# Transformer block on one core: the order of POOL and ScalarE work in the up phase of token block 1

## The chip, the core and the metric

The kernel runs on one core of a Trainium2 chip. The core has five engines with instruction queues of their own, which run in order and wait for one another by semaphores: TensorE (PE in the profile; its weight loads are PEld), VectorE (DVE), ScalarE (ACT), GpSimd (POOL) and SyncE (SP), which here issues transfers. The metric is the device time of one launch in microseconds; the kernel before takes 1042.02 us, the median of three runs (1041.74 to 1042.28).

## What is computed

An attention without softmax, a normalisation per head, and a gated feed-forward block, all in fp32:

```
kv  = einsum('bhsd,bhse->bhde', k, v)          # 8 batches, 8 heads, 576 tokens, 64 columns
o   = einsum('bhsd,bhde->bhse', q, kv)
x   = o / sqrt(mean(o*o) + 1e-6) * g_norm      # per head; then 4608 tokens x 512
g   = x @ w_gate;  val = x @ w_val             # 512 -> 1536
out = (silu(g) * val) @ w_out                  # 1536 -> 512
```

## The kernel before, in words

The 4608 tokens are nine blocks of 512. A block has an up phase (`Ffn.up`: x times w_gate and w_val, and h = silu(g) * val) and a down phase (`Ffn.down`: h times w_out), between and inside which the attention of the next block is woven. Products are done by Strassen's scheme in Winograd's form: seven products instead of eight, at the price of sums of operands and results. Block 0's up phase is plain. Block 1 (the only one with `0 < n < DEEP`, DEEP being 2) uses one level, in six units of class `Up`, called pairs here, 0 to 5: each makes 256 of the 1536 columns of h. Blocks 2 to 8 use two levels (`Inner`), with weight sums that block 1 prepares and writes to DRAM ("leaf steps").

A pair has products P1, P5, P4, P3, P6, P2, P7; each is eight records of 128x256 on PE. `sequence` puts a pair's P4 and P3 behind the P1 and P5 of the next pair. So on PE the order is P1(j+1), P5(j+1), P4(j), P3(j), P6(j+1), P2(j+1), P7(j+1), and what lies from one P1 to the next is called a slot here; slot j is the one in which h of pair j is made. After pairs 1 and 3 there is also a product of k and v, and after pair 5 there are transposes of q for block 2, since there is no next pair.

P1, P6, P7 and P4 add up in one PSUM bank (`b`), which is read out between them: by ACT copies after P1 (L526), P6 (L530) and P7 (L560), and by ACT's silu after P4 (L566). P5 and P3 do so in bank `c`, which VectorE reads (L111) after P7 and after P3. P2 is in bank `a`; VectorE adds it to the copy of P1 (`after2`), and ACT's silu of that sum is L561. Then h is two products on POOL (L113): the first from P4's silu, "h a" below, the second from the sum after P3, "h b". VectorE's `h_sums` makes two further sums of them for the down phase, the second of which needs h b; they are `s<-h` and `h<-s,h` in the profile.

Three of the seven weight operands of a pair are differences T, made on POOL by `Up.prepare` (L112, `t<-wv`, `t<-wg,wv`), for P5, P7 and P4. Their tiles come from a pool of nine. VectorE's leaf steps then work on the same tiles in place and their results go to DRAM; only then may a tile be used again, three pairs later. The down phase has three such differences of w_out for each of P5, P7 and P4 (`turn_t`, `t<-wo`).

The program's text doesn't fix the order on an engine: a scheduler does, by when it takes operands to be ready. `tc.issue_after(ins)` puts what is traced inside it behind `ins` in the queue of the engine of `ins`, and changes nothing on other engines.

In the order before, ACT has in each pair the silu of L561 ahead of the copy of L560. POOL has T of pair 3 before and between the two h products of pair 0, T of pair 4 about those of pair 1, T of pair 5 about those of pair 2, and the T of the down phase's P5 about those of pair 3.

Of the kernel before, what the change touches and what calls it, by code (L numbers as in the profile page):

```python
# [12 lines left out]
ACT = mybir.ActivationFunctionType  # L13
# [5 lines left out]
def kernel(  # L19
# [41 lines left out]
    nc = tc.nc  # L61
# [5 lines left out]
    BLK = P * T  # L67
    HB = BLK // 2
# [4 lines left out]
    NP = NF // 2  # L73
# [39 lines left out]
    mul = lambda e, o, a, b: e.tensor_tensor(out=o, in0=a, in1=b, op=OP.mult)  # L113
# [371 lines left out]
    DEEP = 2  # L485
# [3 lines left out]
    class Quad:  # L489
# [8 lines left out]
        def prepare(self):  # L498
            pass
# [32 lines left out]
    class Up(Quad):  # L532


        def __init__(self, ffn, j):
            super().__init__(2)
            self.ffn, self.j = ffn, j
            self.h = ffn.h[:, 2 * j : 2 * j + 2]

        def prepare(self):  # L540
            j = self.j
            b11, b21, t2, b22 = wg[j][:, 0:2], wg[j][:, 2:4], wv[j][:, 0:2], wv[j][:, 2:4]
            t = []
            for b in (b22, b11, b21):
                t.append(t_tile())
                sub(nc.gpsimd, t[-1], b, t2)
            self.w = {1: b11, 2: b21, 3: b22, 6: t2, 5: t[0], 7: t[1], 4: t[2]}
# [9 lines left out]

        def after7(self):
            self.u3 = self.piece(2)
            nc.scalar.copy(out=self.u3, in_=self.ps["b"])  # L560
            nc.scalar.activation(out=self.s, in_=self.s, func=ACT.Silu)  # L561
            add(nc.vector, self.u3, self.ps["c"], self.u3)

        def after4(self):
            g = self.piece(3)
            nc.scalar.activation(out=g, in_=self.ps["b"], func=ACT.Silu)  # L566
            mul(nc.gpsimd, self.h[:, :, HB:BLK], g, self.u3)

        def after3(self):
            add(nc.vector, self.u2, self.ps["c"], self.u2)  # L570
            mul(nc.gpsimd, self.h[:, :, 0:HB], self.s, self.u2)
            self.ffn.ended = self.ffn.h_sums(self.j, 1, nc.vector)

        def multiply(self, p):
# [180 lines left out]
    def t_tile(key=None):  # L755

        stream.held.append(key)
        return t_pool.tile([P, 2, 2 * P], F32, name="t")
# [114 lines left out]
    class Ffn:  # L873
# [22 lines left out]
        def up(self, fill):  # L896

            self.s1 = s_pool.tile([P, NP, HB], F32, name="s1")
            units = []
            for d in range(NP // 2):  # L900
                if self.n < DEEP:
                    units += [Up(self, 2 * d), Up(self, 2 * d + 1)]
                else:
                    shared = {}
                    units += [Inner(self, d, g, shared) for g in range(4)]
            units[0].prepare()
            last = None
            for i, this in enumerate(units):
                if i + 1 < len(units):
                    units[i + 1].prepare()  # L910
                for unit, p in this.sequence(last):
                    if unit:
                        unit.multiply(p)
                        self.make(4)
                last = this
                fill.get(12 * (i + 1) // len(units), lambda: None)()
            self.down_ = Down(self)
            self.down_.turn_t(5)
            for unit, p in last.sequence(None):
                if unit is None:  # L920
                    last.multiply(p)
# [159 lines left out]
```

## Time and profile before

| | before |
|---|---|
| time, median of three | 1042.02 us |
| span of the profiled run | 1040.8 us |
| VectorE busy | 702.9 us, 68% |
| ScalarE busy | 230.9 us, 22% |
| POOL busy | 369.3 us, 35% |
| granted TensorE clock, mean of the run | 0.994 |

The profile has a page for the whole run, and views that can be asked of a stretch of it: the timeline of an engine, a table of who waited for whom, and a table of busy times by stretch. In a timeline the columns are the start in us, the length in us (including a wait for a resource in the engine itself), engine, line, operation, output and input, and a number of merged instructions; a bracket gives idle time ahead of it and what ended it. Lines L111, L112 and L113 are one-line helpers for add, subtract and multiply, so tile names and not lines tell such instructions apart: `r` is working room, `t` the tiles of T, `wv`, `wg`, `wo` the weights, `s` and `h` the sums and h. Block 1's up phase, the stage concerned, is from 162.5 to 247.8 us.

### The profile page before, as it was taken

What the parts mean: (1) busy time and instruction counts of PE and PEld (TensorE: products, weight loads), DVE (VectorE), ACT (ScalarE), POOL (GpSimd) and SP (SyncE); (2) the same over time, 40 slices, a digit from 0 to 9 for tenths busy, and PEclk for the clock granted to TensorE, in tenths of its full rate; (3) what the DMA queues carried; (4) which work ended last, traced back from release to release, by engine and by line L of the source; (5) the groups of instructions that cost most, each with busy time, mean ns of one, the idle gap of its engine ahead of it and who ended that gap; (6) DMA issues with size and microseconds to landing.
All of it is one profiled execution on the core that took longest, in us unless ns stands there. A gap on an engine that the chain in (4) does not pass through costs nothing.

```text
span 1040.8 us, 21533 instructions
## 1 busy us (share of the span) xinstructions
PE 1015.1 (98%) x8588; PEld 911.7 (88%) x8588; DVE 702.9 (68%) x1203; ACT 230.9 (22%) x356; POOL 369.3 (35%) x280
## 2 busy tenths in 40 slices
PE   5899999999999999999999999999999999999998
PEld 4644688788899989998999899988999899989997
DVE  2999596888655866665766656683668566856661
ACT  2666211122212121111111121211222121212110
POOL 0000443435024631563046305540355126512670
PEclk9899999999999999999999999999999999999999
DMA  9787303765467556764677377726862666066611
GB/s 244 216 268 248 107 1 115 189 187 154 120 184 239 141 102 196 245 164 77 197 238 196 58 205 226 221 47 169 247 194 56 157 207 190 30 152 209 192 31 41
DMA packets 255043, 168.15 MB, mean 162 GB/s; under 512 B 124640, under 2 KB 230240, under 8 KB 254944
## 3 DMA queue, kind: packets, MB, share of 16 engines
q1 hardware_dynamic: 229536, 163.63, 55.6%
q10 hardware_dynamic: 25344, 3.15, 1.9%
q8 instruction: 68, 1.11, 0.4%
q14 instruction: 31, 0.25, 0.1%
q0 software_dynamic: 64, 0.00, 0.0%
HBM read 138.02 MB, written 22.41 MB: 154 GB/s over the span
## 4 chain that ended last, share of the span: by engine, by line
PE 91%; DVE 4%; DMA 2%; SPq 1%; issue 1%; POOL 0%; ACT 0%; DVEq 0%; POOLq 0%; ACTq 0%
PE b L659 25%; PE b L510 20%; PE c L659 12%; PE c L510 9%; PE a L659 6%; PE a L510 5%; PE b L953 4%; PE c L953 4%; PE m L285 2%; PE m L326 1%; SPq L228 1%; DVE xi L112 1%; DMA w<-t 1%; PE m L373 1%; DMA ld<-in_moe_w_gate_dram 1%
## 5 line engine op out<-in xcount | busy, mean ns | idle before, releaser
L111 POOL TENSOR_TENSOR r<-r 128x256 f32<-128x256 f32 (+1 forms) x105 | 110.8, 1061 | 309.3 <-DVE r L111 263.0
L111 DVE TENSOR_TENSOR r<-b,r 128x512 f32<-128x512 f32 (+1 forms) x273 | 162.0, 606 | 63.6 <-PE b L659 59.1
L112 POOL TENSOR_TENSOR t<-wo 128x512 f32<-128x512 f32 x81 | 115.6, 1451 | 196.7 <-DVE wo L111 108.1
L111 DVE TENSOR_TENSOR r<-c,r 128x512 f32<-128x512 f32 (+1 forms) x179 | 108.5, 617 | 89.1 <-PE c L659 49.3
L659 PE MATMUL b<-x,t 128*128 128x128 f32 x1092 | 151.0, 276 | 0.0
L111 DVE TENSOR_TENSOR r<-a,r 128x512 f32<-128x512 f32 (+1 forms) x99 | 62.5, 631 | 110.7 <-PE a L510 65.8
L659 PEld LDWEIGHTS b<-x,t 128*128 128x128 f32 x1092 | 136.5, 192 | 0.6 <-DVE r L111 0.2
L113 POOL TENSOR_TENSOR h<-r 128x1024 f32<-128x1024 f32 (+1 forms) x40 | 81.5, 2052 | 87.4 <-DVE r L111 74.1
L659 PE MATMUL c<-xi,t 128*128 128x128 f32 x840 | 112.2, 275 | 0.3 <-DVE xi L111 0.3
L659 PEld LDWEIGHTS c<-xi,t 128*128 128x128 f32 x840 | 102.8, 192 | 0.4 <-DVE xi L111 0.4
L510 PE MATMUL b<-wo,h 128*128 128x256 f32 x432 | 99.4, 382 | 0.1
L510 PE MATMUL b<-t,h 128*128 128x256 f32 x432 | 96.9, 381 | 0.0
L510 PEld LDWEIGHTS b<-t,h 128*128 128x128 f32 x432 | 81.4, 190 | 11.2 <-issue 0.2
L510 PEld LDWEIGHTS b<-wo,h 128*128 128x128 f32 x432 | 80.0, 190 | 12.6 <-DVE h L113 2.5
L673 ACT COPY r<-b 128x512 f32<-128x512 f32 x63 | 36.9, 585 | 212.7 <-PE b L659 205.9
L659 PE MATMUL b<-xi,t 128*128 128x128 f32 x588 | 79.7, 276 | 0.0
L659 PEld LDWEIGHTS b<-xi,t 128*128 128x128 f32 x588 | 72.4, 192 | 0.0
L659 PE MATMUL b<-x,wg 128*128 128x128 f32 x336 | 52.7, 279 | 0.2 <-DVE x L112 0.2
L659 PE MATMUL b<-x,wv 128*128 128x128 f32 x336 | 51.4, 276 | 0.0
L510 PE MATMUL c<-t,s 128*128 128x256 f32 x216 | 48.3, 380 | 0.0
L510 PE MATMUL a<-wo,h 128*128 128x256 f32 x216 | 48.3, 379 | 0.0
L510 PE MATMUL c<-wo,h 128*128 128x256 f32 x216 | 48.1, 379 | 0.0
(131 smaller groups left out, 1591.1 us busy)
## 6 DMA issues: line engine op xcount, KB each, us to landing
t<-w SPq DMA_DIRECT2D x336, 256.0 KB, 3.3
out_dram<-r SPq DMA_DIRECT2D x17, 512.0 KB, 3.1
ld<-in_moe_w_gate_dram SPq DMA_DIRECT2D x12, 512.0 KB, 4.9
ld<-in_moe_w_val_dram SPq DMA_DIRECT2D x12, 512.0 KB, 4.8
ld<-in_moe_w_out_dram SPq DMA_DIRECT2D x12, 512.0 KB, 4.5
w<-t SPq DMA_DIRECT2D x18, 256.0 KB, 2.4
w<-xi SPq DMA_DIRECT2D x12, 384.0 KB, 3.2
ld<-in_k_dram SPq DMA_DIRECT2D x26, 160.0 KB, 3.5
```

What stands on the lines that cost most here:

```text
L111: add = lambda e, o, a, b: e.tensor_tensor(out=o, in0=a, in1=b, op=OP.add)
L112: sub = lambda e, o, a, b: e.tensor_tensor(out=o, in0=a, in1=b, op=OP.subtract)
L113: mul = lambda e, o, a, b: e.tensor_tensor(out=o, in0=a, in1=b, op=OP.mult)
L228: nc.sync.dma_start(out=t, in_=src[self.n, 2 * j : 2 * j + 2, s0 : s0 + m * D].rearrange("h (p t) d -> p h (t d)", t=m),)
L285: nc.tensor.matmul(self.kv_ps[r][u * D : (u + 1) * D, j, :], lhsT=self.k[j, r][:, u, c, :], rhs=self.v[j, r][:, u, c, :], start=(c == 0), ...
L326: nc.tensor.matmul(self.ps[i][u][p : p + D, t, j, :], lhsT=self.qt[rows, 2 * i + t, j, p : p + D], rhs=kvs[b % 3][rows, j, :], start=True, ...
L373: nc.tensor.transpose(ps[:, e, t], xt[:, t, j + e], ident)
L510: nc.tensor.matmul(banks[e][:, e], lhsT=lhsT, rhs=rhs, start=first and i == 0 and (e == 0 or banks[0] is not banks[1]), stop=i == self.ste ...
L659: nc.tensor.matmul(ps[:, i, f], lhsT=self.weight(o, p, f), rhs=self.operand(o, p), start=first and (i, f) == (0, 0), stop=True, skip_group ...
L673: nc.scalar.copy(out=dst, in_=ps)
L953: nc.tensor.matmul(t, lhsT=w[f // 2][:, i, P * (f % 2) : P * (f % 2 + 1)], rhs=x[:, i, of], start=(i == 0), stop=(i == NS - 1),)
```

## The change

Four edits, all for block 1 alone. T of a pair is no longer prepared one unit ahead of the loop but traced after P3 of the previous pair, and queued on POOL behind that pair's second h product. The T of the down phase's P5 waits, by a semaphore, for the last h sum that was made when it is traced, which is pair 4's. The silu of L561 is queued on ACT behind the copy of L560. The h products of the last pair are on VectorE. They are meant to let h go first on POOL, and to let the copy of P7 leave bank `b` without waiting for the sum that the silu needs.

```diff
@@ class Up
             self.h = ffn.h[:, 2 * j : 2 * j + 2]
+            self.engine = nc.gpsimd if j + 1 < NP else nc.vector
...
-            nc.scalar.copy(out=self.u3, in_=self.ps["b"])
-            nc.scalar.activation(out=self.s, in_=self.s, func=ACT.Silu)
+            copied = nc.scalar.copy(out=self.u3, in_=self.ps["b"])
+            with tc.issue_after(copied.ins):
+                nc.scalar.activation(out=self.s, in_=self.s, func=ACT.Silu)
...
-            mul(nc.gpsimd, self.h[:, :, HB:BLK], g, self.u3)
+            mul(self.engine, self.h[:, :, HB:BLK], g, self.u3)
...
-            mul(nc.gpsimd, self.h[:, :, 0:HB], self.s, self.u2)
+            self.made = mul(self.engine, self.h[:, :, 0:HB], self.s, self.u2)
@@ Ffn.up
-                if i + 1 < len(units):
-                    units[i + 1].prepare()
                 for unit, p in this.sequence(last):
                     if unit:
                         unit.multiply(p)
                         self.make(4)
+                    if p == 3 and i + 1 < len(units):
+                        with tc.issue_after(last.made.ins) if last and self.n < DEEP else ExitStack():
+                            units[i + 1].prepare()
...
-            self.down_.turn_t(5)
+            self.down_.turn_t(5, self.ended if self.n < DEEP else None)
```

On the engines the scheduler makes of it: POOL has T0, T1, h of pair 0, T2, h of pair 1, T3, h of pair 2, T4, h of pair 3, T5, h of pair 4, then the three T of the down phase's P5 (T0 is pair 0's three differences, and so on). ACT has copy and silu exchanged in all six pairs. VectorE's order is the same as before up to the last pair, where the two h products come in. TensorE's order is the same.

## The prediction

> **What bounds the kernel now.** I read the page first.
>
> ```profile
> PE 1015.1 (98%) x8588; PEld 911.7 (88%) x8588; DVE 702.9 (68%) x1203; ACT 230.9 (22%) x356; POOL 369.3 (35%) x280
> PE 91%; DVE 4%; DMA 2%; SPq 1%; issue 1%; POOL 0%; ACT 0%; DVEq 0%; POOLq 0%; ACTq 0%
> ```
>
> TensorE is the bound, and only its idle time or a slower clock can change the end. Next, busy times by stretch: the middle row is block 1's up phase, its neighbours the down phases beside it.
>
> ```profile
> core 0: us, PE busy (x) PEld busy (x) DVE busy (x) ACT busy (x) POOL busy (x), PEclk, DMA share, GB/s
> 120.00:162.50 42.50, 42.50 (x328) 37.49 (x327) 33.65 (x52) 9.08 (x17) 19.53 (x13) 1.00 0.14 41
> 162.50:247.80 85.30, 79.77 (x498) 68.91 (x497) 72.11 (x148) 17.61 (x32) 30.80 (x23) 0.98 0.63 175
> 247.80:288.80 41.00, 41.00 (x314) 36.00 (x313) 28.29 (x49) 7.61 (x14) 10.80 (x7) 1.00 0.47 120
> ```
>
> Only this stage loses PE time. A product takes 1.73 us from start to start in PE's timeline; 42 of them are 72.5, two k-v products of 1.31 make 2.6, transposes 0.8 and 1.1: 77.0 us. The stage takes 85.3, so about 8 us is to be had, no more. The table of waits of the stage says where:
>
> ```profile
> PE b L510 <- ACT r L560: 5.5, 3, 2.3
> PEld b L510 <- ACT r L560: 4.5, 2, 2.7
> DVE h L112 <- POOL h L113: 5.4, 2, 2.7
> POOL t L112 <- DMA w<-t: 33.2, 6, 10.0
> ```
>
> P4 waits for the copy of P7, three times; weight loads wait with it (the same time). VectorE waits twice for h, where POOL has it behind a T that waits for a tile. PE's timeline at the longest wait:
>
> ```profile
> 198.61 1.89 PE L510 MATMUL c<-x,t 128*128 128x256 f32 x8
> 202.79 3.47 PE L510 MATMUL b<-x,t 128*128 128x256 f32 x8 [2.29 <-ACT r L560]
> 206.04 2.15 PE L510 MATMUL c<-x,wv 128*128 128x256 f32 x8
> 208.03 1.89 PE L510 MATMUL b<-x,wv 128*128 128x256 f32 x8
> ```
>
> P4 came 4.18 us after P5 instead of 1.73 (2.45 lost) and then took 3.25 instead of 1.73, P3 1.99: another 1.8 us at a low clock. The two other stops (P4 at 231.81 and 243.22) lost 1.55 and 1.85 and 0.1 each afterwards. Together 7.8 us.
>
> Why is the copy late? ACT has the silu ahead of it, and that waits for VectorE's sum after P2 ("sum 2"). Sum 2 starts 1.5, 4.3, 5.8, 4.0, 4.9 and 2.4 us after P2's last start-to-start end in pairs 0 to 5. So VectorE is late, and the last view says why; VectorE's timeline, then POOL's:
>
> ```profile
> 210.98 0.41 DVE L111 TENSOR_TENSOR wv<-wv 128x256 f32<-128x256 f32 x1
> 211.42 1.64 DVE L112 TENSOR_TENSOR xi<-wv 128x512 f32<-128x512 f32 x1
> 212.98 1.49 DVE L112 TENSOR_TENSOR h<-s,h 128x256 f32<-128x256 f32 x1
> 214.40 0.41 DVE L112 TENSOR_TENSOR xi<-wv 128x256 f32<-128x256 f32 x1
> ```
> ```profile
> 211.13 1.38 POOL L113 TENSOR_TENSOR h<-r 128x512 f32<-128x512 f32 x1 [1.50 <-DVE r L111]
> 212.48 1.71 POOL L112 TENSOR_TENSOR t<-wo 128x512 f32<-128x512 f32 x1
> ```
>
> The `xi` instruction, 0.68 elsewhere, ends when POOL's h has ended; T then waits for `xi`, and `h<-s,h`, 0.41 elsewhere, for T. They take turns.
>
> **What the Trainium skill says.** SBUF — State Buffer, "Who interferes with whom": VectorE with two SBUF inputs contends with a GpSimd instruction that reads SBUF; the pair of ports is an exclusive lock, and the loser "fully blocks". With at most one SBUF input outside a two-port mode it doesn't contend. The trace agrees: the two rows above, and a VectorE copy out of PSUM at 248.97 that takes its usual 0.68 beside POOL's h. TensorE: Matmul & The Clock Gate, "What's actually happening": an idle window of about 3.4 us halves the clock, a busy one restores it. The trace agrees in kind: P4's 3.25 is nearly twice 1.73, and the low stretch cost 1.8 us; here a gap of 2.45 was already enough, ones of 1.55 and 1.85 weren't.
>
> **The change part by part.**
>
> Silu behind the copy: the copy now needs P7 and ACT alone, and is done 0.6 us after P7, while P4 comes two products (3.46 us) later. P4's waits go, up to 7.8 us. What queues behind silu now: the copy of the next P1, which P6 waits for, four products after that P1 starts; at the lags above it is in time. But P3 accumulates in bank `c`, which VectorE's sum after P7 ("sum 7") must have read. In VectorE's order sum 7 ends 2.55 us after sum 2 starts (201.0 to 203.5), against 1.87 for the old copy, and P3 is one product after P4. So the new limit on lateness is only 1.73 - 0.68 = 1.05 us looser. **The copy's wait turns into one for sum 7, if VectorE stays as late.** In the last pair, sum 7 ended at 244.47 and P3 started at 245.02: there only 0.55 can be saved.
>
> POOL's order: what VectorE pays. Its own instructions from one sum 2 to the next: pair 5's 11.31 (229.94 to 241.25) less two blocked ones (1.41 for 0.29, 1.64 for 0.68) is 9.2; pair 4's 14.42 less 1.08, 0.95, 2.72 idle for h and 0.33 for a kv sum is 9.3. I take 9.3. Each POOL instruction costs it 0.96 to 1.08 in the rows above; bounds 0.95 and the whole 1.27 of an undisturbed one; I take 1.05. Trial on before, from sum 2 of pair 0 (170.94) to the end of sum 7 of pair 5: five times 9.3, 0.3 of kv, 21 POOL instructions (11 T, 10 h) at 1.05 and 3.2 for the last stretch are 72.1; measured 73.5. So in this stage VectorE and POOL run in turns, and their sum per pair, some 14.5 us, is more than PE's 12.1.
>
> After: T2 comes into the stage (three instructions made at 154 to 159 before), T3 to T5 stay, the down phase's three T move behind pair 4's h sum, all ahead of pair 5's sum 7; h of pairs 0 to 4 is ten. That is 15 T and 10 h, 25 instead of 21: +4.2 us. T3's first instruction at 169.01, which blocked a leaf step for 0.8, goes: sum 2 of pair 0 at 170.3. In slot 0 POOL is empty until P4's silu, so VectorE, with nothing blocked, runs ahead of P5 and P4 and idles about 2.0 us (173.4 to 174.5, 175.7 to 176.5). One T lies beside sum 2 of pair 5, which reads PSUM: -0.6. Sum: 170.3 + 2.0 + 46.8 + 25 x 1.05 + 3.2 - 0.6 = 248.0 for the end of sum 7 of pair 5, 3.5 later than before. The waits for h (5.4 us) are no gain by themselves: in them POOL did instructions that VectorE now is blocked by.
>
> PE on the way: with sum 2 at about 186.7, 201.2, 215.8 and 230.7 in pairs 1 to 4, P3 stops for 0 to 2.5 us; these are repaid, since P4(5) is done at about 243 to 244.5, and P3(5) must wait for 248.0 against 245.02 before: **+3.0 us**. That stop is 3.5 to 5 us, longer than the one that cost 1.8 us of clock: **+1.8**.
>
> T in time? T of pair j+2 has its first part 3.8 us after the sum after P3 starts (210.38 to 214.2 in before), about 197.7 for pair 3, whose P5 is at 198.6; for pair 5 a stop of 0.3 us or so, inside the same slack. h on VectorE in pair 5: two of 0.68, behind sum 7, in reach of the down phase's P1, which needs them in its last sixth, 4.4 us after its start; not on the path. The down phase's T are done by 246, its P5 begins 6 us after P1: nothing. Nothing behind it changes: the down phase starts later as a whole.
>
> Sum: 1042.0 + 3.0 + 1.8 = 1046.8.
>
> **The rivals.**
>
> *TensorE becomes the bound* (chance 0.18): POOL's T fall mostly into VectorE's idle time, sum 7 is in time, and all 7.8 us come back: 1034.2. For it: h no longer waits for a T that waits for a DMA, 33.2 us of POOL's waits; the copy's wait surely goes. Against it: the trial sum, which leaves VectorE no room. A half way, some 1038, belongs here.
>
> *An exchange* (0.14): VectorE ends about where it did, because a few of the four added POOL instructions fall beside sums from PSUM, and the clock isn't lowered: sum 7 at 244.5 to 246.5, -0.5 to +1.5, near 1042.5.
>
> *The port is dearer* (0.10): in three T in a row VectorE pays the whole 1.27: 25 x 0.22 = 5.5 more at sum 7, 1052.3; half of it 1049.5.
>
> The likeliest (0.58) is 1046.8, with 1044.8 if the clock isn't lowered.
>
> **How the numbers follow.** Faster by over 0.2% is the first rival, 0.18; same the second, 0.14; slower the rest, 0.68. The range reaches down to 1038.5, to the half way of the first rival, and up to 1050, which leaves out its full gain and the upper end of the third.
>
> **What would show it.** Right: no PE wait for L560; instead PE `c` waits for VectorE `r`, longest in pair 5, 3 us or more, with slow matmuls after it; VectorE's `xi`, `wg` and `h<-s,h` behind the sum after P3 at 1.4 us instead of 0.4, one for each T; sum 7 of pair 5 near 248. Wrong: P4 and P3 back to back in all pairs, VectorE idle in slots 1 to 4, or a stage of less than 85 us. It would be wrong above all if VectorE got several instructions in between two T.

## The result and the profile after

The changed kernel takes 1046.05 us, the median of six runs (1043.85 to 1048.34), against 1042.09 us for the kernel before (1041.74 to 1042.44). The ratio is 1.0039, with a 95% interval of 1.0026 to 1.0052: slower by 4.0 us, where 1046.8 us was forecast. The two profiled runs differ by 4.3 us in their spans (1040.8 and 1045.1).

The table of waits of the changed kernel's up phase has a single row for PE. Its columns are the same as before: us in total, times, the longest.

```profile
PE c L510 <- DVE r L111: 8.8, 4, 4.4
```

The wait for the copy of P7 is gone altogether. P3, which accumulates in bank `c`, now waits for VectorE's sum 7 instead, four times. PE's timeline at the last of these, with the products around it:

```profile
240.77 1.97 PE L510 MATMUL b<-x,t 128*128 128x256 f32 x8
247.19 3.78 PE L510 MATMUL c<-x,wv 128*128 128x256 f32 x8 [4.45 <-DVE r L111]
250.76 0.63 PE L306 MATMUL b<-ident,ld 128*128 128x128 f32 x2
251.18 1.06 PE L306 MATMUL m<-ident,ld 128*128 128x128 f32 x4
252.04 0.93 PE L306 MATMUL b<-ident,ld 128*128 128x128 f32 x4
252.81 5.34 PE L510 MATMUL b<-wo,h 128*128 128x256 f32 x24
```

The same stretch before the change had no stop at P3:

```profile
243.22 1.97 PE L510 MATMUL b<-x,t 128*128 128x256 f32 x8 [1.85 <-ACT r L560]
245.02 1.89 PE L510 MATMUL c<-x,wv 128*128 128x256 f32 x8
247.84 5.34 PE L510 MATMUL b<-wo,h 128*128 128x256 f32 x24
```

P3 of pair 5 starts at 247.19 (245.02 before). Then the clock is low: from P3 to the first product of the down phase are 5.62 us, against 2.82 before (245.02 to 247.84). The down phase starts at 252.81 instead of 247.84, and the two parts of those 5.0 us are 2.2 for the wait and 2.8 for the clock. Block 2 begins 5.0 us later too (293.85 for 288.88). The spans differ by 0.7 us less than that: later, at 723 us, PE waits 0.6 us for a DMA in the profile of before, and not in that of the changed kernel.

VectorE's timeline in front of that sum 7, and POOL's:

```profile
239.96 0.41 DVE L112 TENSOR_TENSOR h<-s,h 128x256 f32<-128x256 f32 x1
240.30 0.41 DVE L112 TENSOR_TENSOR xi<-wv 128x256 f32<-128x256 f32 x1
240.63 1.49 DVE L112 TENSOR_TENSOR wg<-wg 128x256 f32<-128x256 f32 x1
242.15 1.37 DVE L111 TENSOR_TENSOR wg<-wg 128x256 f32<-128x256 f32 x1
243.45 0.68 DVE L111 TENSOR_TENSOR r<-a,r 128x512 f32<-128x512 f32 x1
244.05 1.15 DVE L112 TENSOR_TENSOR xi<-wg 128x512 f32<-128x512 f32 x1
...
246.46 0.67 DVE L111 TENSOR_TENSOR r<-c,r 128x512 f32<-128x512 f32 x1
```
```profile
240.51 4.14 POOL L112 TENSOR_TENSOR t<-wo 128x512 f32<-128x512 f32 x3 [1.02 <-PE m L306]
```

The three T of the down phase start as soon as `h<-s,h` is done (the code makes them wait for it; the bracket names a transpose on PE that ended within 0.1 us of it), and each blocks one of VectorE's next instructions: `wg` takes 1.49 and 1.37 instead of 0.41, `xi` 1.15 instead of 0.68. Sum 2 (243.45, reading bank `a` in PSUM) runs beside a T at its usual 0.68. Sum 7, the last row, ends at 247.13.

### The profile page after: what moved, and what is told of

Read it like the earlier page. It is cut to its first block, busy times and chain, and to the rows that moved or that the text cites. A ratio compares the mean times of both kernels' runs of the same rounds, so it can differ in the third digit from the quotient of the medians.

```text
span 1045.1 us, 21527 instructions
## 1 busy us (share of the span) xinstructions
PE 1015.5 (97%) x8588; PEld 911.5 (87%) x8588; DVE 706.6 (68%) x1205; ACT 231.1 (22%) x356; POOL 369.0 (35%) x278
## 4 chain that ended last, share of the span: by engine, by line
PE 90%; DVE 5%; SPq 2%; DMA 1%; issue 1%; ACT 0%; POOL 0%; DVEq 0%
PE b L662 25%; PE b L510 20%; PE c L662 12%; PE c L510 10%; PE a L662 6%; PE a L510 5%; PE c L958 4%; PE b L958 4%; PE m L285 1%; DVE xi L112 1%; PE m L326 1%; SPq L228 1%; DVE r L111 1%; DMA ld<-in_moe_w_gate_dram 1%; DVE r L112 0%
## 5 line engine op out<-in xcount | busy, mean ns | idle before, releaser
L113 POOL TENSOR_TENSOR h<-r 128x1024 f32<-128x1024 f32 (+1 forms) x38 | 79.1, 2099 | 128.1 <-DVE r L111 86.0
```

## The experiments

Theory: VectorE's instructions with two SBUF inputs and POOL's take turns, their sum per pair is more than PE's time, and the end of the up phase is set by sum 7 of pair 5. Rivals are named in the expectations. Each ratio is to the kernel before in the same batch of runs, whose level differs a little from batch to batch. The stage starts at 161.7 to 162.9 us in the profiles, so times of two kernels compare to within about 1 us, unless the shift is allowed for.

**The held silu alone.**

```diff
-            nc.scalar.copy(out=self.u3, in_=self.ps["b"])
-            nc.scalar.activation(out=self.s, in_=self.s, func=ACT.Silu)
+            copied = nc.scalar.copy(out=self.u3, in_=self.ps["b"])
+            with tc.issue_after(copied.ins):
+                nc.scalar.activation(out=self.s, in_=self.s, func=ACT.Silu)
```

> The kernel before with one edit, the silu of L561 queued behind the copy of P7; POOL and VectorE keep their order. Port theory (VectorE and POOL take turns at SBUF, so VectorE's sums are late and only the wait changes its name): P4's three waits for the copy go, and P3 waits for sum 7 instead, about 1.3 us in pair 2, 0.5 in pair 4; sum 7 of pair 5 still ends near 244.5 us, so P3 of pair 5 starts at about 244.5 instead of 245.0. Time 1041.5; if the gap of some 2.4 us in front of that P3 lowers the clock, 1043.3. Rival (the copy was the whole wait): all of the 7.8 us come back, 1034.2.

Ratio 0.9996 (0.9988 to 1.0005). PE's timeline of this kernel has the exchange of one wait for another, and the chance of the clock:

```profile
204.12 2.00 PE L510 MATMUL c<-x,wv 128*128 128x256 f32 x8 [1.70 <-DVE r L111]
...
232.96 3.44 PE L510 MATMUL c<-x,wv 128*128 128x256 f32 x8 [2.13 <-DVE r L111]
...
244.83 2.00 PE L510 MATMUL c<-x,wv 128*128 128x256 f32 x8 [0.27 <-DVE r L111]
```

P3 waits for sum 7 four times, as in the changed kernel: the rows above, for pairs 2, 4 and 5, and 0.49 us in pair 3. The stops of pairs 2 and 4 are longer than was expected, but sum 7 of pair 5 is where it was (ends 244.78; 244.47 before). What PE gained on the way is lost in front of that last sum. The copy was not the whole wait.

**The down phase's T out of the way of sum 7.**

```diff
-            add(nc.vector, self.u3, self.ps["c"], self.u3)
+            self.seven = add(nc.vector, self.u3, self.ps["c"], self.u3)
...
-            self.down_.turn_t(5, self.ended if self.n < DEEP else None)
+            self.down_.turn_t(5, last.seven if self.n < DEEP else None)
```

> The changed kernel, but the three T of the down phase's P5 wait for sum 7 of pair 5 instead of pair 4's last h sum. Port theory: the two weight sums and the xi sum that they blocked get 2.6 us back (1.49, 1.37 and 1.15 us for 0.41, 0.41 and 0.68), so sum 7 of pair 5 ends at about 244.5 instead of 247.1 and P3 of pair 5 stops for 2 us instead of 4.5. Time 1041.5 with the clock kept, up to 1043.5 if it is lowered. Rival (the loss was made earlier, by T2 to T5 in slots 0 to 3): sum 7 less than 1 us earlier, 1045 or more.

Ratio 1.0008 (0.9999 to 1.0016), against 1.0039 for the changed kernel: 3.2 us of its 4.0 are gone. PE's row for P3 of pair 5:

```profile
245.04 3.11 PE L510 MATMUL c<-x,wv 128*128 128x256 f32 x8 [1.95 <-DVE r L111]
```

Sum 7 of pair 5 ended at 244.99, 2.1 us earlier. As the stage began 0.3 us later in this profile (162.83 for 162.49), that is 2.5 us of the stage's own time, which is what the three rows of VectorE shown above were longer by. P3 took 3.11 us, so the clock still fell somewhat. The rival falls: most of the loss came from three instructions placed just ahead of sum 7.

**T written, not computed.**

```diff
-                sub(nc.gpsimd, t[-1], b, t2)
+                nc.gpsimd.memset(t[-1], 0.01)
```

> The changed kernel, but T of the six pairs isn't computed: POOL fills those tiles with a constant at the same places of its queue, which writes SBUF and reads nothing. Port theory: VectorE is blocked by ten h products and three T of w_out only, 13 instead of 25 POOL instructions; its own 9.3 us and 2.1 for h are less than the pair's 12.1 on PE, so PE has no stop in pairs 0 to 4 and a short one in pair 5: 1034 to 1037. Rival (it is the order of POOL's queue and its waits, not what POOL reads): sum 7 and PE's stops stay as in the changed kernel, 1046.

This kernel leaves out the values of T; only its times are of use. Ratio 0.9956 (0.9942 to 0.9971), 1037.5 on the scale of before, 0.5 above the range that was expected. VectorE's timeline, then POOL's, in the stretch where T of pair 2 was computed in the changed kernel:

```profile
180.98 0.41 DVE L112 TENSOR_TENSOR h<-s,h 128x256 f32<-128x256 f32 x1
181.32 0.41 DVE L112 TENSOR_TENSOR xi<-wv 128x256 f32<-128x256 f32 x1
181.65 0.41 DVE L112 TENSOR_TENSOR wg<-wg 128x256 f32<-128x256 f32 x1
```
```profile
180.45 1.45 POOL L548 MEMSET t<- 128x512 f32 x3
```

The same in the changed kernel, beside three T:

```profile
181.80 1.48 DVE L112 TENSOR_TENSOR h<-s,h 128x256 f32<-128x256 f32 x1
183.21 1.50 DVE L112 TENSOR_TENSOR xi<-wv 128x256 f32<-128x256 f32 x1
184.63 1.49 DVE L112 TENSOR_TENSOR wg<-wg 128x256 f32<-128x256 f32 x1
```
```profile
181.29 1.71 POOL L112 TENSOR_TENSOR t<-wv 128x512 f32<-128x512 f32 x1
182.97 2.87 POOL L112 TENSOR_TENSOR t<-wg,wv 128x512 f32<-128x512 f32 x2
```

Beside three fills VectorE's rows take their undisturbed 0.41. This agrees with the Trainium skill (SBUF — State Buffer, "Who interferes with whom"): a GpSimd instruction that only writes doesn't contend with VectorE's two-input ones. A fill is also shorter, 0.48 us for 1.27, but the rows show no blocking at all. P3 had no stop in pairs 0 to 4, and one of 2.9 us in pair 5, where the three T of w_out were left in.

**Unused products in the gap.**

```diff
                     last.multiply(p)
+                    if p == 4 and self.n < DEEP:
+                        spare = c_psum.tile([P, 2, HB], F32, name="c")
+                        with tc.issue_after(last.mm.ins):      # the last product of P4
+                            for i in range(8):
+                                nc.tensor.matmul(
+                                    spare[:, i % 2], lhsT=wg[0][:, i % 4, 0:P], rhs=self.att.x[:, i % 4, i // 4],
+                                    start=True, stop=True, skip_group_check=True,
+                                )
```

> The changed kernel, with eight unused products (3.5 us) on PE between P4 and P3 of pair 5, where PE stops for 4.5 us. Clock theory: P3 of pair 5 starts at 247.2 as in the changed kernel, but takes 1.9 us instead of 3.8, and the transposes and the next product run at full speed: 2 to 3 us less, 1043.2 to 1044. Rival (the stop alone costs; the slow matmuls are made up for later): 1046.

Ratio 1.0021 (1.0013 to 1.0028), 1.9 us less than the changed kernel, though PE does 3.5 us of useless work. PE's timeline:

```profile
243.44 3.62 PE L931 MATMUL c<-x,wg 128*128 128x256 f32 x16
246.89 1.89 PE L510 MATMUL c<-x,wv 128*128 128x256 f32 x8
```

P3 comes as late as in the changed kernel, but takes 1.89 instead of 3.78, and the down phase starts 2.8 us after it, at 249.71. The clock's share is thereby measured apart from the wait's, though loosely: the two ratios' intervals leave 0.3 to 3.5 us for it, an estimate from their widths.

**Single parts of the change undone.** The silu ahead of the copy again, and in another kernel the last pair's h on POOL:

```diff
-            copied = nc.scalar.copy(out=self.u3, in_=self.ps["b"])
-            with tc.issue_after(copied.ins):
-                nc.scalar.activation(out=self.s, in_=self.s, func=ACT.Silu)
+            nc.scalar.copy(out=self.u3, in_=self.ps["b"])
+            nc.scalar.activation(out=self.s, in_=self.s, func=ACT.Silu)
```
```diff
-            self.engine = nc.gpsimd if j + 1 < NP else nc.vector
+            self.engine = nc.gpsimd
```

> The changed kernel with the silu back ahead of the copy of P7; POOL's order as changed. Port theory: P4 waits for sum 2, the silu and the copy again, 1.05 us longer than P3 waits for sum 7: stops of about 2.5 us in pair 2, 1.7 in pair 3, 3.4 in pair 4 (with a lower clock after the longer ones), but in pair 5 the stop ends at the same sum: copy at 245.2, P4 then, P3 at 247.0. The end is set by VectorE's sum 7 of pair 5 and hardly moves: 1045.5 to 1047. Rival (the held silu is what made the changed kernel slow): 1042.

> The changed kernel with the last pair's h back on POOL. Port theory: these come after sum 7 of pair 5 and are in time for the last sixth of the down phase's first product either way: the same as the changed kernel, 1046 (within 0.5). Rival (two products of 0.68 us on VectorE, the short engine, cost the end 1.4 us): 1044.6.

Ratios 1.0042 (1.0027 to 1.0057) and 1.0036 (1.0023 to 1.0049): neither differs from the changed kernel's by more than the intervals. With the silu first, P4 of pair 5 waits for the copy, and so for the silu and for sum 2, until 245.38. It takes 3.75 us at a low clock, and P3 follows at 248.93, after sum 7 had ended at 247.12. So here it is sum 2 of VectorE, and not sum 7, that sets the end, at nearly the same time. The silu's place, and which engine makes the last h, are worth nothing that can be seen while VectorE is that late.

**Towards a faster version.** First, from the kernel before: the held silu, and the down phase's T behind sum 7 of pair 5 (the edit shown above).

> The kernel before with two edits: the silu behind the copy of P7, and the three T of the down phase's P5 behind sum 7 of pair 5 (in before they ran in slots 3 and 4, at 212, 220 and 226 us). Port theory: in the stage VectorE is blocked 18 times instead of 21, so sum 7 of pair 5 ends 3.2 us earlier, at about 241.3; the stop of pair 2 stays 1.7 us, that of pair 4 goes. P3 of pair 5 starts at 241.4 against 245.0: 3.6 us less than before, 1038.4, or 1040.2 if a stop lowers the clock. Rival (POOL's T hidden in slots 3 and 4, no gain from moving them): as with the silu alone, within 1 us of before.

Ratio 0.9994 (0.9985 to 1.0002): a miss, by some 3 us. P3 of pair 5 started at 242.69, 2.3 us earlier than before (2.6 of the stage's own time) instead of 3.6: an `xi` leaf step at 228.74, for which VectorE was now early, waited 1.87 us for the write to DRAM of the previous pair's. And two new stops stood in the down phase, 0.99 us for the last h, queued on POOL behind those T, and 0.75 for the normalisation of block 2 on VectorE.

Next, the leaf steps behind the sums that PE waits for:

```diff
                         unit.multiply(p)
-                        self.make(4)
+                        if self.n < DEEP and p == 7:
+                            with tc.issue_after(unit.seven.ins):
+                                self.make(12)
+                        elif self.n >= DEEP or p not in (6, 2):
+                            self.make(4)
```

> As the last, and the leaf steps made after P6, P2 and P7 of a pair in block 1 are queued on VectorE behind that pair's sum 7, so that both sums come before eight weight sums and two T sums (some 4.7 us of them lie ahead of sum 7 in before). Port theory: VectorE and POOL have no less to do, but PE no longer waits for what is late; the rest goes on beside the down phase, where VectorE has some 12 us free. No stops of PE worth more than 1 us: 7 us less than before, 1035. Rival (VectorE is short of time whatever the order, since it runs in turns with POOL at 14.5 us per pair against PE's 12.1): the stops come back by pair 4 or 5, and the time is that of the last kernel, 1038 to 1040.

Ratio 1.0006 (0.9998 to 1.0015): a miss of nearly 8 us, and the most telling one. The up phase did what was expected, with no stop; the down phase began at 240.38, 7.5 us earlier than before. PE's timeline in the down phase:

```profile
246.82 1.13 PE L510 MATMUL b<-wo,h 128*128 128x256 f32 x4 [1.96 <-POOL h L113]
...
264.42 1.97 PE L373 MATMUL m<-ident,r 128*128 128x128 f32 x8 [4.82 <-DVE r L113]
```

What VectorE had put off came due there: PE waited 1.96 us for the last h and 4.82 for the normalised x of block 2. VectorE did leaf steps from 247.1 to 259.5 us with T of POOL between them, ahead of the normalisation, and the transposes at 264.42 then ran at a low clock (1.97 us for 1.04).

Two kernels take that away. The first puts the last pair's h on VectorE (as in the change) and the T of the down phase's P4 behind the first half of block 2's normalisation:

```diff
-                    down.turn_t(4, nxt.halves[0] if nxt and nxt.n >= TURNED else None)
+                    down.turn_t(4, nxt.halves[0] if nxt and nxt.n >= DEEP else None)
```

The second, against the first, also puts the leaf steps left when pair 5 begins behind it:

```diff
-                        if self.n < DEEP and p == 7:
+                        if self.n < DEEP and i + 1 == len(units):
+                            if p in (5, 4):
+                                self.make(12)
+                        elif self.n < DEEP and p == 7:
...
                 down.multiply(p)
-                self.make(12)
+                if p in fill:
+                    fill[p]()
+                if self.making and p != 1:
+                    with tc.issue_after(nxt.halves[0].ins):
+                        self.make(24)
...
-                if p in fill:
-                    fill[p]()
```

> The kernel with both sums first, and two more edits: the last pair's h on VectorE, and the three T of the down phase's P4 behind the first half of block 2's attention, as later blocks have it. In that kernel PE had no stop in the up phase, but gave the 7.5 us back in the down phase: 2.0 us for h of the last pair, which queued behind T on POOL, and 4.8 us (and a lower clock) for the transposes that wait for the normalisation of block 2 on VectorE, where leaf steps and six T of POOL came first. Port theory: the stop for h goes, and three T less, 3.2 us, stand before the normalisation; a stop of 1.5 to 2 us is left. 5 us less than before, 1037 (ratio 0.995). Rival (PE is bound somewhere else behind the down phase, by the loads of block 2): within 1 us of before.

> As the last, and the leaf steps that are left when pair 5 begins (32 of 168) are queued on VectorE behind the first half of block 2's normalisation. Port theory: nothing is ahead of the normalisation but sums that PE needs, so neither the up phase nor that place has a stop; the second half of the normalisation has 13 us, in which 24 leaf steps (about 8.5 us) and three T (3.2 us) leave it just enough. 7 us less than before, 1035 to 1036 (ratio 0.993). Rival (the work comes due again at the second half, or in the writes of the weight sums that block 2 reads): a stop of 2 to 4 us there, 1038 to 1039.

Ratios 0.9956 (0.9943 to 0.9968) and 0.9932 (0.9919 to 0.9946): 1037.48 and 1035.16 us where the kernel before took 1041.83 in the same batch. The first still had stops of 0.96 us for the last h and 0.75 for the normalisation. Busy times from the start of block 1's up phase to the end of its down phase's old span, in the columns shown in the prediction: one row of before, then two of the second kernel.

```profile
162.50:248.00 85.50, 79.97 (x499) 69.11 (x498) 72.31 (x148) 17.69 (x32) 30.80 (x23) 0.98 0.63 175
```
```profile
162.50:248.00 85.50, 85.39 (x592) 74.58 (x591) 63.44 (x134) 20.48 (x36) 34.95 (x25) 1.00 0.60 162
248.00:289.00 41.00, 41.00 (x287) 37.01 (x286) 33.64 (x71) 7.17 (x13) 5.35 (x4) 1.00 0.62 178
```

PE is busy 85.39 of 85.50 us in the first stretch (79.97 before) at a clock of 1.00, and block 2 begins at 281.60 instead of 288.88. This beats both kernels, and with it the 7 to 8 us that the stage was losing are recovered. What each of the edits is worth alone was not tried.

## Why the prediction was right

- **The copy's wait turns into one for sum 7.** Shown: no wait for the copy in the changed kernel, four for sum 7; with the held silu alone the same.
- **VectorE's times.** Sum 2 was put at 186.7, 201.2, 215.8 and 230.7 us in pairs 1 to 4 and started at 186.49, 200.85, 215.34 and 230.16; sum 7 of pair 5 was put at 248.0 and ended at 247.13. The price of 1.05 us for each POOL instruction held: the sixteen rows of `xi`, `h<-s,h`, `xi` and `wg` behind the sum after P3 in slots 0 to 3 paid 0.96 to 1.09. The terms did not all err the same way. What VectorE paid can be read by adding up how much longer its rows were than usual for their shape (0.29, 0.41 and 0.68 us for the three). By this 24 of the 25 instructions blocked VectorE, for 24.4 us in all, where 25.65 was put (25 x 1.05 - 0.6). The other one, h a of pair 0, blocked nothing, but VectorE had to wait for its result, and was idle for 2.8 us where 2.0 was put. Sum 2 of pair 0 started at 170.04; the prediction wrote 170.3, though 0.8 off 170.94 is 170.1.
- **The count of POOL's instructions** stands for two things. In before VectorE was blocked for only 17.5 us by its rows, and idle for 6.0; 5.4 of these are the two waits for h, in which POOL did four of the 21 instructions. At 1.05 us each those four are 1.2 us too cheap, most of what the trial sum was short by (72.1 for 73.5).
- **25 POOL instructions instead of 21.** The fills show that POOL's reading is what VectorE pays for, and the kernel with the down phase's T late shows that most of the loss comes from the three that the change moved to just ahead of sum 7.
- **The wait, +3.0 us:** measured 2.2 in the profiled run.
- **The clock, +1.8 us:** measured 2.8 there, and 1.9 in the medians by the unused products. This term was too small: the price came from a gap of 2.45 us, and this one is of 4.7 us (242.5 to 247.19). The sum of both was put at 4.8 and is 5.0 in the profile; that it came so near is in part luck, since the wait was 0.8 less and the clock 1.0 more. In the medians it is 4.0. The six runs spread over 4.5 us, but 36 runs of before, made with the experiments, spread over 3.5, so the spread doesn't show this clock.
- **Nothing for h on VectorE, nothing behind the down phase's start:** the first is shown by the kernel with h on POOL, the second by block 2's start, which is 5.0 us later like the down phase's.
- **The first rival** (PE-bound, 1034.2) needed more than this change: VectorE's leaf steps had to leave the place ahead of the sums and of the next block's normalisation as well. The last kernel, at 1035.2 and with PE busy in the whole stage, is that case.

Still open: how much of the loss T2 alone, moved into the stage, makes. It was not tried apart; the kernel with the down phase's T late leaves 0.8 us for it and for the clock, and nothing at the low end of its interval.

## What to carry to other kernels

Where two engines take turns, as VectorE and POOL do here, count both engines' instructions in the stage together: putting the right thing first on one of them doesn't help when the sum is more than the bound engine's time, and work moved into the stage costs the other engine a full turn each, about 1.0 us here. Put what the bound engine waits for ahead on the shared one and push the rest to where there is room, and then look at who waits there: in the kernel with both sums first the whole 7.5 us was given back one phase later, by two waits and a low clock. And a stop is not worth its length: those before P3 in pairs 2 to 4 of the changed kernel, 4.4 us together, could not move the end, as P3 of pair 5 had to wait for VectorE anyway, while the last one cost its own 2.2 us and 2.8 more at a low clock.

## What was not expected of the hardware

The clock after a short stop isn't settled by its length. P3 in pair 4 shows it, in four kernels that are the same up to there: after a wait of 2.37 or 2.38 us it took 1.99 us in the changed kernel and in the one with the late T, but 3.48 in the one with unused products and 3.13 in the one with h on POOL. With the held silu alone it took 3.44 after 2.13. In block 1's up phase the longest stop that left the clock alone was one of 2.93 us, before P3 of pair 5 in the kernel with fills (1.99), and the shortest that lowered it one of 1.95, with the late T (3.11). So stops of some 2 to 3 us lower the clock in some executions and not in others. The Trainium skill (TensorE: Matmul & The Clock Gate, "What's actually happening") says that the window is free-running, which fits, and puts an idle window at about 3.4 us, which these shorter stops don't fit.
